# A linear-attention layer and two mixture-of-experts layers on one core: other steps, rows and counts in the attention stage

## The chip, the core and the metric

One core of one Trainium2 chip runs the whole program in one launch. The metric is device time in microseconds (us), the median of several runs. A core has five engines that run side by side, each with its own in-order list of instructions: TensorE (PE, matrix products), VectorE (DVE), ScalarE (ACT), GpSimd (POOL) and SyncE (SP, which here only starts transfers). An engine stops at an instruction whose inputs are not there, and everything behind it in its list stops too.

## What is computed

An attention with a decaying state is followed by a layer that sends each of 1536 tokens to the best of 8 experts, and by a second such layer with a capacity per expert.

```python
def _attn_ref(r, k, v, w, u):                      # 2 batches, 8 heads, 768 steps, 48 wide
    for t in range(S):
        cur = np.einsum('bhd,bhe->bhde', u[None] * kt, vt)
        y[:, :, t] = np.einsum('bhd,bhde->bhe', rt, state + cur)
        state = wt[:, :, :, None] * state + np.einsum('bhd,bhe->bhde', kt, vt)
...
def _moe_ref(x, ...):                              # 1536 x 384, 8 experts, 1024 hidden
    logits = x @ w_gate + modality_bias[modality_id]
    e_idx = np.argmax(logits, axis=1)
    ...
        h = np.maximum(x[mask] @ w1[e], 0.0)
        out[mask] = gate_w[mask, None] * (h @ w2[e])
```

## The kernel before, in words

**Attention.** The 16 heads are taken two at a time: 8 pairs (0 to 7), each of 6 chunks of 128 steps, so 48 chunk steps in all, one behind the other. For a pair, PE turns w, k and r (`turn`, three chunks to one PSUM tile, three such tiles in rotation); ACT copies w and r out of PSUM, DVE copies k out and multiplies it on the way (L270). DVE runs two scans over w: S (L282) and J (L290 to L292). r is multiplied by J (L297, `mul_r`) on the engine that the string `MR` names for the pair: v is DVE, g is POOL. POOL multiplies r, k and u (L321, L322) and later v (L329) for the diagonal term, whose sums DVE makes (L328).

For two chunks at a time `front` forms the products pa (L373, one PSUM tile only), and DVE masks them into Am (L376). For one chunk `out_y` adds the state's part (L415) and Am's part (L418) in PSUM, and DVE adds two chunks of it to zv (L421). `state` forms the next state: PE adds k times v (L391) in the PSUM tile endt. The string `STATE` says for each chunk of a pair how the old state X comes in. With p, PE adds it through a product with the identity (L393) and ACT scales the sum into the new X (L403). With v, DVE adds X to endt (Z, L398) and scales the sum (L401).

**Order.** All engines run in the order in which the code is written. The table `PLAN` says for each pair at which third of which chunk step each of its sixteen parts is written; `PRE`, `PLAN0` and `FRONT` do so for pair 0, with `F` and a number for that many products of ones (L524, `filler`), whose result nobody reads. `XTURN`, `XTURN2` and `XLOG` place the turns of finished rows and the expert logits of the first nine groups of 128 tokens; `SLOT` places single jobs.

**Choosing two experts early.** Once the first batch's logits are known, `Pick.find` counts its tokens per expert, finds the two experts with most tokens, and SP loads their weights while attention still runs (`RawWeights.first`, L966, L959, L961). Its DVE steps are written one or two to a chunk step (`pull`), from the chunk step `SLOT["pick"]` on.

**Behind attention** come the routing of the first expert layer (L785 on), that layer, a second routing and the second layer. Nothing there is touched by the change, but for the tiles that `Pick` hands over (`at`, `force`, `upto`, `hop`), which keep their meaning.

Of the kernel before, what the change touches and what calls it, by code (L numbers as in the profile page):

```python
# [59 lines left out]
XTURN = ((1, 0, 3, 5, 6, 7), (2, -2, 0, -1, 4, 4))  # L60
XTURN2 = ((2, 3, 4, 6, 7, 8), (2, 3, 5, 99, 99, 99))
# [68 lines left out]
class Pick:  # L130


    def __init__(self, nc, c, g, oh, psum):
        self.nc, self.c, self.oh, self.psum = nc, c, oh, psum
        self.T = lambda nm, shape, dt=F32: g.tile(shape, dt, name="pk_" + nm)
        self.one = []
        self.at = self.T("at", [1, 2])
        self.ati = self.T("ati", [1, 2], I32)

    def find(self):  # L140

# [9 lines left out]
        at = T("atm", [1, 2, E])  # L151
        num = c.jx[:, 0:E]
        for i in range(2):
            mx, eq, cum = T(f"mx{i}", [P, 1]), T(f"eq{i}", [P, E]), T(f"cum{i}", [P, E])
            one = T(f"one{i}", [P, E])
# [7 lines left out]
            self.one.append(one)  # L163
# [3 lines left out]
        a, b = self.one  # L167
# [1339 lines left out]
```

## Time and profile before

| | |
|---|---|
| median of 3 runs | 474.61 us (472.51 to 476.15) |
| the profiled execution's own time | 473.01 us, of which the profile's span is 471.3 us |
| PE busy | 429.7 us, 91% |
| DVE busy | 346.9 us, 74% |
| ACT busy | 239.4 us, 51% |
| POOL busy | 150.3 us, 32% |

Times in the views count from the start of the span. Attention runs from the start to about 128.8 us, the first routing to about 141.7 us, and the two expert layers to the end. A busy share says little by itself: PE's products take longer when its clock is granted at half, and then it is busy for longer with the same work. So the granted clock (PEclk, 1.00 for 2.4 GHz, 0.50 for 1.2 GHz) is read beside PE's list, and each gap in that list is read with what ended it.

### The profile page before, as it was taken

How to read it: one execution, taken by the hardware profiler on the slowest of the kernel's cores; microseconds unless marked ns; L12 is line 12 of the kernel's file. 1: busy time of each engine (PE TensorE's matmuls, PEld its weight loads, DVE VectorE, ACT ScalarE, POOL GpSimd, SP SyncE). 2: the span in 40 equal slices, each digit the busy share in tenths (PEclk: the TensorE clock that was granted, in tenths of full speed). 3: DMA queues.
4: the chain of work that ended last, by engine and by line, in shares of the span. 5: the costliest groups of instructions: out<-in, count | busy, mean ns of one | idle time of the engine just before them, and what ended most of it. 6: DMA issues, size and time to landing. Idle time of an engine off the chain costs nothing. (4 is left out here: it accounts for less than half of the span.)

```text
span 471.3 us, 9450 instructions
## 1 busy us (share of the span) xinstructions
PE 429.7 (91%) x3188; PEld 389.5 (83%) x3188; DVE 346.9 (74%) x669; ACT 239.4 (51%) x472; POOL 150.3 (32%) x159
## 2 busy tenths in 40 slices
PE   7989999979979899999999787898999999999990
PEld 4778878868739899999999776388899999998990
DVE  7787977994288984865947587889989559569770
ACT  3335353522344473654745464545857547568560
POOL 5528767230032032021220331243533221224500
PEclk9979999995799999999999889899999999999996
DMA  6966538108632022137772763431597676684200
GB/s 114 200 110 121 100 60 202 30 2 329 230 110 69 2 69 73 37 106 223 259 231 74 208 207 117 160 87 35 206 312 269 203 232 234 184 250 130 54 10 25
DMA packets 83989, 66.82 MB, mean 142 GB/s; under 512 B 58986, under 2 KB 76055, under 8 KB 83904
## 3 DMA queue, kind: packets, MB, share of 16 engines
q1 hardware_dynamic: 78912, 52.26, 37.4%
q0 software_dynamic: 4992, 13.53, 10.1%
q8 instruction: 42, 0.69, 0.6%
q14 instruction: 43, 0.35, 0.2%
HBM read 95.55 MB, written 11.51 MB: 227 GB/s over the span
## 5 line engine op out<-in xcount | busy, mean ns | idle before, releaser
L1007 DVE TENSOR_TENSOR w1l<-w1r,w1h 128x512 fp32r<-128x512 f32 x120 | 75.2, 683 | 0.8 <-ACT w1h L1004 0.7
L1007 DVE TENSOR_TENSOR w2l<-w2r,w2h 128x768 fp32r<-128x768 f32 x80 | 71.9, 949 | 0.7 <-ACT w2h L1004 0.5
L1004 ACT CAST w1h<-w1r 128x512 fp32r<-128x512 f32 x120 | 66.2, 621 | 7.2 <-DMA w2r<-in_moe_w_dram 6.2
L1004 ACT CAST w2h<-w2r 128x768 fp32r<-128x768 f32 x80 | 61.5, 838 | 0.0
L1133 ACT ACTIVATE qhh_m<-qh_m 128x512 fp32r<-128x512 f32 x48 | 28.7, 599 | 62.5 <-PE qh_m L1128 58.9
L1134 DVE SCALAR_TENSOR_TENSOR qhl_m<-qh_m,qhh_m 128x512 fp32r<-128x512 f32 x48 | 32.9, 686 | 28.4 <-ACT qhh_m L1133 27.8
L1128 PE MATMUL qh_m<-xh,w1h 128*128 128x256 f32 x288 | 51.6, 288 | 0.5 <-PE lpl_y_m L710 0.3
L1157 POOL DMA_INDIRECT x<-yo,ids_l x14 | 15.1, 1080 | 115.6 <-DVE yo L1154 66.0
L1128 PE MATMUL qh_m<-xl,w1h 128*128 128x256 f32 x288 | 50.2, 283 | 0.1
L1128 PE MATMUL qh_m<-xh,w1l 128*128 128x256 f32 x288 | 49.8, 282 | 0.0
L1157 POOL DMA_INDIRECT out_dram<-yo,ids_l x20 | 24.9, 1244 | 67.7 <-DVE w1l L1007 17.8
L1128 PEld LDWEIGHTS qh_m<-xh,w1h 128*128 128x128 f32 x288 | 42.3, 188 | 1.1 <-ACT xh L1337 0.8
L1046 POOL DMA_INDIRECT xg<-x,idg_l x24 | 28.1, 1170 | 45.8 <-PE xp_m L1061 32.4
L1128 PEld LDWEIGHTS qh_m<-xl,w1h 128*128 128x128 f32 x288 | 41.0, 189 | 0.5 <-DVE w2l L1007 0.5
L1128 PEld LDWEIGHTS qh_m<-xh,w1l 128*128 128x128 f32 x288 | 40.9, 188 | 0.0
L403 ACT ACTIVATE X<-endt,Sb 112x112 f32<-112x112 f32 x32 | 11.3, 354 | 50.9 <-PE endt L393 37.2
L1046 POOL DMA_INDIRECT xg<-xs,idg_l x20 | 22.7, 1136 | 34.9 <-DVE ec_l L888 29.1
L418 PE MATMUL py<-raw_v,Am 128*128 128x96 f32 x192 | 32.7, 299 | 0.0
L1062 ACT CAST xh<-xp_m 128x384 fp32r<-128x384 f32 x38 | 16.7, 485 | 27.9 <-PE xp_m L1061 26.6
L418 PEld LDWEIGHTS py<-raw_v,Am 128*128 128x128 f32 x192 | 29.5, 220 | 0.1
L1146 PE MATMUL qy_m<-w2h,qhh_m 128*128 128x384 f32 x96 | 25.6, 348 | 0.0
L1146 PE MATMUL y_m<-w2h,qhh_m 128*128 128x384 f32 x96 | 25.1, 342 | 0.0
(281 smaller groups left out, 964.7 us busy)
## 6 DMA issues: line engine op xcount, KB each, us to landing
w2r<-in_moe_w_dram SPq DMA_DIRECT2D x50, 768.0 KB
w1r<-in_moe_w_dram SPq DMA_DIRECT2D x72, 512.0 KB
xs<-zv SPq DMA_DIRECT2D x12, 192.0 KB
out_dram<-zt SPq DMA_DIRECT2D x4, 576.0 KB
raw_w<-in_w_dram SPq DMA_DIRECT2D x14, 144.0 KB
raw_r<-in_r_dram SPq DMA_DIRECT2D x14, 144.0 KB
raw_k<-in_k_dram SPq DMA_DIRECT2D x14, 144.0 KB
raw_v<-in_v_dram SPq DMA_DIRECT2D x14, 144.0 KB
```

The lines of the kernel that those rows point to most:

```text
L403: nc.scalar.activation(Xn, z, AF.Identity, scale=Tn)
L418: nc.tensor.matmul(py[:, 1 - h : 4 - h : 2, 0:D], lhsT=Am[:, h], rhs=vc[:, ch, :, 0:D], start=not ch, stop=True, skip_group_check=True)
L1004: (eng.copy if eng is nc.scalar else eng.tensor_copy)(p[1], p[0])
L1007: eng.tensor_sub(p[2], p[0], p[1].bitcast(F32))
L1046: nc.gpsimd.indirect_dma_start(out=m.xg[j % 2][:, t, 0:SW], out_offset=None, in_=src, in_offset=bass.IndirectOffsetOnAxis(ap=R.idg[:, 2 * ...
L1062: nc.scalar.copy(m.xh[j % 2][:, :, ts], pt)
L1128: nc.tensor.matmul(ph[:, f], lhsT=w[s][:, kc, fs], rhs=a[s][:, kc], start=(i == 0), stop=(i == 3 * KD - 1))
L1133: nc.scalar.activation(hh, ph, AF.Relu)
L1134: nc.vector.scalar_tensor_tensor(hl, ph, 0.0, hh.bitcast(F32), ALU.max, ALU.subtract)
L1146: nc.tensor.matmul(st["y", j, t], lhsT=a[:, f, ts], rhs=w[s][:, 2 * q + f], start=(q == 0 and i == 0), stop=(q == 3 and i == 5))
L1157: nc.gpsimd.indirect_dma_start(out=dst, out_offset=bass.IndirectOffsetOnAxis(ap=R.ids[:, 2 * j + t : 2 * j + t + 1], axis=0), in_=m.yo[j % ...
```

## The change

Five kinds of edit, all in the attention stage:

- `STATE` is ppppp in place of pppvp: for the fourth chunk of each of the 8 pairs, the old state comes in through PE and ACT and no longer through DVE.
- `MR` gives r times J of pairs 2, 4, 5 and 6 to DVE, and that of the others to POOL (before, pairs 1 to 7 were POOL's). Pair 0 is done on DVE in both.
- `Pick.find` joins count and expert number in one value (8 times the count plus the number), takes the two largest with one MAX and their places with one MAX_INDEX, and starts 5 chunk steps later. SP reads the places directly.
- The number and places of the products of ones: 35 in place of 32 for pair 0, and 3 more later.
- `PLAN`, `PRE`, `XTURN`, `XTURN2`, `XLOG` and `SLOT` write the same parts in another order.

```diff
 STEPS = ("w0", "w1", "r0", "S", "r1", "J", "k0", "mr", "k1", "mk", "K0", "K1", "u0", "u1", "c0", "c1")
-PLAN = {1: {'w0': -15, 'w1': -16, 'r0': -15, 'S': -15, 'r1': -13, 'J': -13, 'k0': -12, 'mr': -8, ...
+PLAN = {1: {'w0': -16, 'w1': -17, 'r0': -14, 'S': -16, 'r1': -12, 'J': -14, 'k0': -14, 'mr': -5, ...
-PRE = ('F6', 'n0', 'w0', 'w1', 'F0', 'A', 'S0', 'J0', 'r0', 'F0', 'A', 'm0', 'k0', 'S1', 'F8', 'r1', 'F2', 'J1', 'm1', 'K0', 'F1', 'k1', 'F6')
-FRONT = {0: 3, 1: 6}
-PLAN0 = {0: ('F0', 'n1', 'K1', 'F0', 'u', 'F0'), 3: ('A',), 1: ('U',), 10: ('c0',), 14: ('c1',)}
-MR = 'vggggggg'
-STATE = 'pppvp'
+PRE = ('F6', 'n0', 'w0', 'w1', 'F5', 'A', 'S0', 'J0', 'r0', 'F0', 'A', 'm0', 'k0', 'S1', 'F5', 'r1', 'F3', 'J1', 'm1', 'K0', 'F5', 'k1', 'F0')
+FRONT = {1: 7, 13: 2, 20: 1}
+PLAN0 = {0: ('F2', 'n1', 'K1', 'F0', 'u', 'F2'), 3: ('A',), 1: ('U',), 10: ('c0',), 14: ('c1',)}
+MR = 'ggvgvvvg'
+STATE = 'ppppp'
-SLOT = {'consts': 21, 'small': 9, 'pick': 27, 'xs': 29, 'flag': 44}
+SLOT = {'consts': 17, 'small': 10, 'pick': 32, 'xs': 26, 'flag': 44}
...
-        self.ati = self.T("ati", [1, 2], I32)
+        self.index = self.T("index", [P, 8], mybir.dt.uint32)
+        self.ati = self.index.bitcast(I32)
...
-        yield v.tensor_copy(n, pc)
...
-        for i in range(2):
-            yield v.tensor_reduce(mx, n, AX.X, ALU.max)
-            yield v.tensor_scalar(eq, n, mx, None, ALU.is_equal)
-            yield v.tensor_tensor_scan(cum, c.first[:, 0], eq, 0.0, ALU.mult, ALU.add)
-            yield v.scalar_tensor_tensor(one, cum, 1.0, eq, ALU.is_equal, ALU.mult)
-            if i == 0:
-                yield v.scalar_tensor_tensor(n, one, -2.0 * N, n, ALU.mult, ALU.add)
-            yield v.tensor_tensor(at[:, i], one[0:1], num[0:1], ALU.mult)
-        yield v.tensor_reduce(self.at, at, AX.X, ALU.add)
-        yield v.tensor_copy(self.ati, self.at)
+        yield v.scalar_tensor_tensor(n, pc, float(E), num, ALU.mult, ALU.add)
+        yield v.max(top, n)
+        yield v.max_index(self.index, top, n)
+        yield v.tensor_copy(self.at, self.index[0:1, 0:2])
         yield "at"
-        yield v.tensor_add(self.force, a, b)
-        yield v.tensor_sub(key, b, a)
+        yield v.tensor_scalar(self.force, n, top[:, 1:2], None, ALU.is_ge)
+        yield v.tensor_scalar(key, n, top[:, 0:1], None, ALU.is_equal)
+        yield v.scalar_tensor_tensor(key, n, top[:, 1:2], key, ALU.is_equal, ALU.subtract)
```

The lines of the changed kernel stand 9 lines higher behind `Pick.find` (L373 becomes L364).

**First place: PE, chunk steps 2 and 3 of pair 0.** In a name the digit is the pair (pk_1 is the turned k of pair 1); endt is the state, py the output. Before:

```order
L267 MATMUL pk_1_366<-ident,raw_k_113 112x128 x3
L415 MATMUL py_0_371<-X_0_311,rT_213 128x112
L418 MATMUL py_0_371<-raw_v_111,Am_0_285 128x2x48 x2
L391 MATMUL endt<-raw_v_111,KT_246 48x48 x2
L267 MATMUL pw_2_381<-ident,raw_w_116 112x128 x3
L267 MATMUL pw_2_386<-ident,raw_w_116 112x128 x3
L415 MATMUL py_0_371<-X_0_349,rT_213 128x112
L418 MATMUL py_0_371<-raw_v_111,Am_0_285 128x2x48 x2
L391 MATMUL endt<-raw_v_111,KT_246 48x48 x2
L393 MATMUL endt<-X_0_379,ident 112x112
L267 MATMUL pk_1_408<-ident,raw_k_113 112x128 x3
```

The same place in the changed kernel:

```order
L258 MATMUL pk_1_359<-ident,raw_k_113 112x128 x3
L258 MATMUL pr_1_369<-ident,raw_r_114 112x128 x3
L406 MATMUL py_0_378<-X_0_314,rT_218 128x112
L409 MATMUL py_0_378<-raw_v_111,Am_0_284 128x2x48 x2
L382 MATMUL endt<-raw_v_111,KT_249 48x48 x2
L384 MATMUL endt<-X_0_346,ident 112x112
L258 MATMUL pw_2_387<-ident,raw_w_116 112x128 x3
L258 MATMUL pw_2_392<-ident,raw_w_116 112x128 x3
L406 MATMUL py_0_378<-X_0_346,rT_218 128x112
L409 MATMUL py_0_378<-raw_v_111,Am_0_284 128x2x48 x2
L382 MATMUL endt<-raw_v_111,KT_249 48x48 x2
L384 MATMUL endt<-X_0_385,ident 112x112
```

The product with the identity now stands behind the first pair of L391 too. The next row in the changed kernel is the turn pk_1_409, whose PSUM tile was pk_1_359's.

**Second place: DVE at the same time.** Before:

```order
L292 SCALAR_TENSOR_TENSOR Jf_356<-wb_149,d1f_150 112x774
L270 TENSOR_TENSOR kT_365<-pk_1_366,Sb_333 112x384
L398 TENSOR_TENSOR Z_0_377<-endt,X_0_349 112x112
L401 TENSOR_SCALAR X_0_379<-Z_0_377,Sb_207 112x112
L421 TENSOR_TENSOR zv_156<-py_0_371,zv_156 128x2x96
L308 TENSOR_REDUCE ck<-Sb_207 112x1
L270 TENSOR_TENSOR kT_365<-pk_1_408,Sb_333 112x384
```

The same place in the changed kernel, up to the first Am of pair 1:

```order
L283 SCALAR_TENSOR_TENSOR Jf_354<-wb_149,d1f_150 112x774
L261 TENSOR_TENSOR kT_358<-pk_1_359,Sb_328 112x384
L412 TENSOR_TENSOR zv_156<-py_0_378,zv_156 128x2x96
L299 TENSOR_REDUCE ck<-Sb_212 112x1
L261 TENSOR_TENSOR kT_358<-pk_1_409,Sb_328 112x384
L273 SCALAR_TENSOR_TENSOR Sb_420<-wb_147,d1r 112x774
L367 TENSOR_TENSOR Am_1_438<-pa_1_433,mask 128x512
```

Z and X are gone from DVE; the scan S of pair 2 (L273) now stands ahead of pair 1's first Am.

**Third place: DVE from the second to the third Am of pair 6**, where the last pair's scan J and the choice of experts meet. Before:

```order
L376 TENSOR_TENSOR Am_6_1302<-pa_6_1297,mask 128x512
L290 TENSOR_SCALAR tcl_153<-Sb_1268 112x6
L291 RECIPROCAL d1f_150<-tcl_153 112x6
L292 SCALAR_TENSOR_TENSOR Jf_1308<-wb_149,d1f_150 112x774
L156 TENSOR_REDUCE pk_mx_1312<-pk_n 128x1
L157 TENSOR_SCALAR pk_eq_1313<-pk_n,pk_mx_1312 128x8
L158 SCALAR_TENSOR_TENSOR pk_cum_1314<-first,pk_eq_1313 128x8
L308 TENSOR_REDUCE ck<-Sb_1268 112x1
L421 TENSOR_TENSOR zv_157<-py_6_1317,zv_157 128x2x96
L159 SCALAR_TENSOR_TENSOR pk_one_1315<-pk_cum_1314,pk_eq_1313 128x8
L376 TENSOR_TENSOR Am_6_1345<-pa_6_1340,mask 128x512
```

In the changed kernel:

```order
L367 TENSOR_TENSOR Am_6_1279<-pa_6_1274,mask 128x512
L281 TENSOR_SCALAR tcl_153<-Sb_1265 112x6
L282 RECIPROCAL d1f_150<-tcl_153 112x6
L283 SCALAR_TENSOR_TENSOR Jf_1300<-wb_149,d1f_150 112x774
L261 TENSOR_TENSOR kT_1304<-pk_7_1305,Sb_1265 112x384
L153 SCALAR_TENSOR_TENSOR pk_n<-pk_pc,jx 128x8
L412 TENSOR_TENSOR zv_157<-py_6_1290,zv_157 128x2x96
L154 MAX pk_top<-pk_n 128x8
L367 TENSOR_TENSOR Am_6_1324<-pa_6_1318,mask 128x512
```

Between the scan and the last Am stood six small steps, four of them of the choice that read SBUF alone; now four steps stand there, of which one (MAX) reads SBUF alone.

## Rows read from the trace of the kernel before

**Rows 1.** Granted clock by stretch, attention: stretch, us, PE busy (count), PEclk, DMA

```profile
26.10:32.10 6.00, 6.00 (x31) 0.50 0.59 113
32.10:101.00 68.90, 65.75 (x666) 1.00 0.45 95
103.10:124.20 21.10, 20.64 (x118) 0.52 0.71 263
```

**Rows 2.** PE in time, first gap: start, duration, instruction [idle before <-releaser]

```profile
24.84 0.29 PE L391 MATMUL endt<-raw_v,KT 128*48 128x48 f32 x4 [2.12 <-DVE Z L398]
26.10 0.72 PE L393 MATMUL endt<-X,ident 112*112 112x112 f32 x2 [0.97 <-DVE X L401]
```

**Rows 3.** DVE in time, ahead of the first gap's end

```profile
24.07 0.53 DVE L270 TENSOR_TENSOR kT<-pk,Sb 112x384 f32<-112x384 f32 x1
24.52 0.26 DVE L398 TENSOR_TENSOR Z<-endt,X 112x112 f32<-112x112 f32 x1
24.82 1.23 DVE L401 TENSOR_SCALAR X<-Z,Sb 112x112 f32<-112x112 f32 x1
```

**Rows 4.** POOL in time, at the first gap

```profile
24.30 1.68 POOL L297 TENSOR_TENSOR rT<-rT,Jf 112x768 f32<-112x768 f32 x1 [2.21 <-DMA raw_v<-in_v_dram]
```

**Rows 5.** PE in time, second gap

```profile
103.10 0.71 PE L373 MATMUL pa<-rT,kT 48*128 48x128 f32 x8 [2.08 <-DVE Am L376]
104.28 0.40 PE L391 MATMUL endt<-raw_v,KT 128*48 128x48 f32 x4 [0.46 <-DVE Z L398]
```

**Rows 6.** DVE in time, ahead of the second gap's end

```profile
97.35 1.77 DVE L292 TENSOR_TENSOR_SCAN Jf<-wb,d1f 112x774 f32<-112x774 f32 x1
...
99.47 1.53 DVE L158 TENSOR_TENSOR_SCAN pk_cum<-first,pk_eq 128x8 f32<-128x8 f32 x1
...
101.26 1.10 DVE L159 SCALAR_TENSOR_TENSOR pk_one<-pk_cum,pk_eq 128x8 f32<-128x8 f32 x1
102.28 0.68 DVE L376 TENSOR_TENSOR Am<-pa,mask 128x512 f32<-128x512 f32 x1
```

**Rows 7.** POOL in time, at the second gap

```profile
99.26 1.71 POOL L297 TENSOR_TENSOR rT<-rT,Jf 112x768 f32<-112x768 f32 x1 [6.29 <-DVE pk_mx L156]
100.93 1.40 POOL L321 TENSOR_TENSOR z<-raw_r,raw_k 128x576 f32<-128x576 f32 x1
102.41 1.40 POOL L322 TENSOR_TENSOR z<-z,ub 128x576 f32<-128x576 f32 x1
```

**Rows 8.** PE in time: another gap, and the longest with no fall behind it

```profile
134.79 1.02 PE L860 MATMUL pid_l<-rid_l,ohp_l 128*128 128x26 f16 x12 [1.53 <-DVE ohp_l L858]
277.48 0.47 PE L1080 MATMUL ph_m<-w1h,xh 128*128 128x512 f32 x1 [1.95 <-ACT w1h L1004]
```

**Rows 9.** Granted clock behind the gap that ends at 277.48

```profile
278.00:280.00 2.00, 2.00 (x6) 0.50 0.58 116
```

**Rows 10.** PE in time: two products at the full clock, then at half

```profile
97.42 0.72 PE L373 MATMUL pa<-rT,kT 48*128 48x128 f32 x8
100.43 0.60 PE L418 MATMUL py<-raw_v,Am 128*128 128x96 f32 x4
107.20 1.03 PE L418 MATMUL py<-raw_v,Am 128*128 128x96 f32 x4
108.16 1.23 PE L373 MATMUL pa<-rT,kT 48*128 48x128 f32 x8
```

**Rows 11.** PE in time: products of ones, a product with the identity, its successor

```profile
7.14 1.89 PE L524 MATMUL junk<-fill 128*128 128x512 bf16 x8
...
16.42 0.45 PE L393 MATMUL endt<-X,ident 112*112 112x112 f32 x2
16.70 0.82 PE L267 MATMUL pw<-ident,raw_w 128*112 128x128 f32 x6
```

**Rows 12.** DVE in time: half a pair's r times J, pair 0

```profile
8.01 0.56 DVE L297 TENSOR_TENSOR rT<-rT,Jf 112x384 f32<-112x384 f32 x1
```

**Rows 13.** SP in time: the first load of the chosen experts' weights

```profile
106.11 1.44 SPq L959 DMA_DIRECT2D w1r<-in_moe_w_dram  x3
```

More of the change, by code (lines that the diff above doesn't have):

```diff
@@ new lines @@
+PLAN = {1: {'w0': -16, 'w1': -17, 'r0': -14, 'S': -16, 'r1': -12, 'J': -14, 'k0': -14, 'mr': -5, 'k1': -8, 'mk': -9, 'K0': -6, 'K1': -1, 'u0': -12, 'u1': -4, 'c0': 0, 'c1': 8}, 2: {'w0': -28, 'w1': -27, 'r0': -25, 'S': -24, 'r1': -20, 'J': -22, 'k0': -18, 'mr': -10, 'k1': -10, 'mk': -5, 'K0': -11, 'K1': -1, 'u0': -13, 'u1': -3, 'c0': -9, 'c1': 3}, 3: {'w0': -26, 'w1': -33, 'r0': -26, 'S': -24, 'r1': -19, 'J': -20, 'k0': -16, 'mr': -17, 'k1': -12, 'mk': -11, 'K0': -7, 'K1': 1, 'u0': -16, 'u1': -7, 'c0': -14, 'c1': 0}, 4: {'w0': -33, 'w1': -28, 'r0': -23, 'S': -21, 'r1': -15, 'J': -19, 'k0': -15, 'mr': -9, 'k1': -6, 'mk': -11, 'K0': -14, 'K1': -2, 'u0': -8, 'u1': -4, 'c0': 2, 'c1': 5}, 5: {'w0': -27, 'w1': -31, 'r0': -17, 'S': -22, 'r1': -13, 'J': -15, 'k0': -21, 'mr': -13, 'k1': -5, 'mk': -11, 'K0': -7, 'K1': 0, 'u0': -23, 'u1': -9, 'c0': -12, 'c1': 3}, 6: {'w0': -32, 'w1': -25, 'r0': -23, 'S': -23, 'r1': -22, 'J': -20, 'k0': -20, 'mr': -18, 'k1': -19, 'mk': -11, 'K0': -8, 'K1': -6, 'u0': -20, 'u1': -13, 'c0': -11, 'c1': -10}, 7: {'w0': -29, 'w1': -32, 'r0': -26, 'S': -22, 'r1': -20, 'J': -16, 'k0': -16, 'mr': -10, 'k1': -12, 'mk': -11, 'K0': -14, 'K1': -6, 'u0': -10, 'u1': -1, 'c0': -14, 'c1': -5}}
@@ L57 @@
+FRONT = {1: 7, 13: 2, 20: 1}
+PLAN0 = {0: ('F2', 'n1', 'K1', 'F0', 'u', 'F2'), 3: ('A',), 1: ('U',), 10: ('c0',), 14: ('c1',)}
+MR = 'ggvgvvvg'
+STATE = 'ppppp'
 KD_ = 'dddddddd'
 AHEAD = (3, 1)
-SLOT = {'consts': 21, 'small': 9, 'pick': 27, 'xs': 29, 'flag': 44}
-XTURN = ((1, 0, 3, 5, 6, 7), (2, -2, 0, -1, 4, 4))
-XTURN2 = ((2, 3, 4, 6, 7, 8), (2, 3, 5, 99, 99, 99))
+SLOT = {'consts': 17, 'small': 10, 'pick': 32, 'xs': 26, 'flag': 44}
+XTURN = ((-3, -1, 2, 8, 4, 5), (0, 3, 2, -1, 0, 5))
+XTURN2 = ((2, 3, 4, 8, 6, 5), (5, 1, 4, 99, 99, 99))
@@ L65 @@
 GROUPS = ((0, (0, 1, 2)), (0, (3, 4, 5)), (1, (0, 1, 2)))
-XLOG = (4, 8, 5)
+XLOG = (4, 9, 5)
 EXPERT0 = (0, E - 1)
@@ L135, in __init__ @@
         self.T = lambda nm, shape, dt=F32: g.tile(shape, dt, name="pk_" + nm)
-        self.one = []
         self.at = self.T("at", [1, 2])
-        self.ati = self.T("ati", [1, 2], I32)
+        self.index = self.T("index", [P, 8], mybir.dt.uint32)
+        self.ati = self.index.bitcast(I32)
     def find(self):
         v, c, T = self.nc.vector, self.c, self.T
-        n = T("n", [P, E])
-        yield v.tensor_reduce(n, self.oh[:, :, 0:CH], AX.X, ALU.add)
         half = T("half", [P, E], BF16)
-        yield v.tensor_copy(half, n)
+        with self.nc.allow_low_precision(reason="whole numbers up to six"):
+            ins = v.tensor_reduce(half, self.oh[:, :, 0:CH], AX.X, ALU.add)
+        yield ins
         yield
@@ L149, in find @@
         yield self.nc.tensor.matmul(pc, lhsT=c.ones, rhs=half, start=True, stop=True)
-        yield v.tensor_copy(n, pc)
-        at = T("atm", [1, 2, E])
         num = c.jx[:, 0:E]
-        for i in range(2):
-            mx, eq, cum = T(f"mx{i}", [P, 1]), T(f"eq{i}", [P, E]), T(f"cum{i}", [P, E])
-            one = T(f"one{i}", [P, E])
-            yield v.tensor_reduce(mx, n, AX.X, ALU.max)
-            yield v.tensor_scalar(eq, n, mx, None, ALU.is_equal)
-            yield v.tensor_tensor_scan(cum, c.first[:, 0], eq, 0.0, ALU.mult, ALU.add)
-            yield v.scalar_tensor_tensor(one, cum, 1.0, eq, ALU.is_equal, ALU.mult)
-            if i == 0:
-                yield v.scalar_tensor_tensor(n, one, -2.0 * N, n, ALU.mult, ALU.add)
-            yield v.tensor_tensor(at[:, i], one[0:1], num[0:1], ALU.mult)
-            self.one.append(one)
-        yield v.tensor_reduce(self.at, at, AX.X, ALU.add)
-        yield v.tensor_copy(self.ati, self.at)
+        n, top = T("n", [P, E]), T("top", [P, 8])
+        yield v.scalar_tensor_tensor(n, pc, float(E), num, ALU.mult, ALU.add)
+        yield v.max(top, n)
+        yield v.max_index(self.index, top, n)
+        yield v.tensor_copy(self.at, self.index[0:1, 0:2])
         yield "at"
-        a, b = self.one
         self.force = T("force", [P, E])
-        yield v.tensor_add(self.force, a, b)
+        yield v.tensor_scalar(self.force, n, top[:, 1:2], None, ALU.is_ge)
         key = T("key", [P, E])
-        yield v.tensor_sub(key, b, a)
+        yield v.tensor_scalar(key, n, top[:, 0:1], None, ALU.is_equal)
+        yield v.scalar_tensor_tensor(key, n, top[:, 1:2], key, ALU.is_equal, ALU.subtract)
         yield v.scalar_tensor_tensor(key, key, 2.0 * E, num, ALU.mult, ALU.add)
```

1 line of the change is left out of this document (removed).

## The prediction

> **What bounds the kernel now.** I read the granted clock by stretch first, then PE's own list in order of time with the gap ahead of each row, and then, for each long gap, the lists of the engines that it names. Attention is a stretch of small products on PE, one behind the other, and PE is what it waits for: from 32.10 to 101.00 us PE is busy for 65.75 of 68.90 us at the full clock [rows 1]. Two stretches are different. From 26.10 to 32.10 and from 103.10 to 124.20 us PE is as busy, but at a granted clock of 0.50 and 0.52, half speed [rows 1]. Ahead of each stands a gap. In the first PE waits 2.12 us for Z and then 0.97 us for X, the two DVE steps that bring the old state in [rows 2]. In the second it waits 2.08 us for an Am and then 0.46 us for a Z [rows 5].
>
> A gap costs its own length and, if it is long, the clock behind it. In the whole trace PE has five gaps of 1.95 us and more, and each is followed by half speed (for the shortest, at 277.48 us, the clock is 0.50 just behind it). The longest that isn't is 1.53 us [rows 8, 9]. At half speed the masked product of L418 takes 1.03 us where it took 0.60, and pa 1.23 where it took 0.72 [rows 10]. That is 1.71 times as long, so of each us at half speed 0.41 is lost (1 less 1/1.71). The two stretches hold 6.00 and 20.64 us of busy time [rows 1] and lose 2.5 and 8.5 us. With the gaps (2.12 + 0.97 + 2.08 + 0.46 = 5.6 us) that is 16.6 us of attention's 128.8 in which PE does less than it could.
>
> Why DVE is late is in the lists of DVE and POOL. DVE steps that read SBUF alone, with two inputs or as a plain scale, stand still while POOL multiplies. At 99.47 us an 8-wide scan takes 1.53 us, until POOL's r times J (99.26 us, 1.71 us) is done. The next such step at 101.26 us takes 1.10 us, until POOL's next product (100.93 us, 1.40 us) is done [rows 6, 7]. At 24.82 us the scale of Z takes 1.23 us beside POOL's r times J at 24.30 us [rows 3, 4]. Steps with a PSUM input don't wait: Am at 102.28 us takes 0.68 us although the next POOL product starts at 102.41 us [rows 6, 7].
>
> **First gap.** The change takes Z and X off DVE for all 8 pairs, so PE no longer needs DVE between two chunks. What is late next at this place is kT of pair 1: the turn of its second half goes into the PSUM tile of the first, which DVE reads from 24.07 to 24.60 us [rows 3]. Nothing of DVE's work ahead of it changes, so it stays at 24.60. PE came to the old gap at 24.84 - 2.12 = 22.72 us [rows 2] with the same turns done. In the changed order it has in addition two products with the identity and one pair of L391 to do before it stops (0.28 us each from the start of one to the start of its successor, 16.42 to 16.70 us [rows 11], and no more for the other), 0.8 us, and three more products of ones, 0.65 us (0.216 us each, the start-to-start step in 1.89 us for eight, less the 0.16 us by which the last one ends late [rows 11]). It arrives at about 24.2 us and waits 0.4 us. A little later pa of chunks 2 and 3 of pair 1 needs the Am ahead of it, which now stands behind pair 2's scan S. That scan has to wait for POOL's r times J until 25.98 us [rows 4], takes 1.77 us as J does [rows 6], and Am 0.68: 28.4 us. PE, with six more groups of products of 0.3 to 0.7 us behind 24.6, comes there at about 27.7 and waits 0.7 us. Both waits are short, so no half speed is to follow.
>
> **Second gap.** Between the end of the last pair's scan J (97.35 + 1.77 = 99.12 us) and Am (102.28 us) DVE spent 3.2 us, of which 2.6 in two 8-wide steps held up by POOL [rows 6, 7]. In the changed order four steps stand there: kT (0.53, as at 24.07 us [rows 3]), one that reads PSUM, the sum into zv, and MAX. Only MAX reads SBUF alone. No row shows a MAX: from below it is an 8-wide step of 0.15 us (the 0.6 us that the two held steps leave of the 3.2, over four steps), from above it is held until POOL's r times J ends, as the scan at 99.47 us was, 1.53 us. I take the upper value, because POOL starts that product as soon as J is done. Then Am ends 2.5 us behind the scan, 1.3 us earlier than now (102.96 less 99.12 = 3.8). PE stopped 1.9 us behind the scan (103.10 - 2.08 = 101.02); it now has one product with the identity and one of ones more to do there (0.5 us). On that count alone 0.1 us is left to wait, and DVE, freed of the choice's steps between the Ams of pair 6, enters the stretch without the backlog that it had (Am at 102.28 belongs to a pa that was done at 98.14 us [rows 6, 10]). So the gap goes.
>
> **The other parts.** Eight products with the identity more, on PE, in plain sight: 8 x 0.28 = 2.2 us. Six more products of ones: 6 x 0.216 = 1.3 us; those of pair 0 lie partly in its waits, so the bounds are 0 and 1.3, and I take 1.3. ACT gets eight scales more, as it has them for the other chunks; it is busy for 51% of the span, and each scale has a chunk step's time until its X is read. DVE gets r times J of four pairs: 0.56 us for half a pair [rows 12], so about 1.0 for one, 4 us, against eight times Z and X (0.26 us for Z [rows 3] and, where nothing holds it, as much for X, 4.2 us) and ten steps of the choice (0.15 each, 1.5 us). So DVE has 1.7 us less, and POOL 4 x 1.68 = 6.7 us less [rows 4]. The rest of `PLAN` moves parts by one or two chunk steps; I went through the order pair by pair with these durations and found no wait above 1 us. Turns, logits and stores are as many as before. The choice starts five chunk steps later but has eleven writings less, so the load of the weights is issued at the same place within half a chunk step: 106.11 us now [rows 13], 22.7 us ahead of attention's end. At the full clock it would come about 18 us ahead of that end. Eight transfers, 4.7 MB, are wanted by then, the first five of them first. At the 263 GB/s of the stretch in which they run now [rows 1], a rate that counts time without loads too, they take 18 us at most. That cover gets thin but holds; without it each us late is a us lost.
>
> By a rule of the Trainium skill (GPSIMD Engine Reference, section 8, Key points) GpSimd shares its SBUF interfaces with VectorE and is in contention with its instructions that have two SBUF inputs. The trace agrees, with 1.53 us for an 8-wide scan. It speaks against the four multiplies on DVE: by it each can be held for a POOL product, and the sum would be 4 x 1.40 = 5.6 us worse on DVE. PE would see only what exceeds its lead.
>
> **Sum.** 16.6 us of gaps and half speed go; 2.2 for products with the identity, 1.3 for products of ones and 1.1 for the two new waits come: 12.0 us less. Against the profiled execution's own 473.01 us that is 461.0. The median of the runs is 474.61, 1.6 above it, so 462.6 us. Nothing behind attention changes, and the gain is handed through to the end, since routing and the expert layers start when the last logits are there.
>
> **Rivals.** *One long gap is left.* DVE or POOL is late at one more place, most likely where DVE has r times J of pair 6 behind scan J and two kT (about 4.8 us of DVE work between two Ams, against 3.5 us of PE work), or at MAX, if POOL's three products run through without letting it in (4.5 us [rows 7]). For it: POOL's products did hold DVE through. Against it: DVE comes to both places with a lead, as the sums above show for MAX. The rule on the shared interfaces, in the Trainium skill's page named above, would bring this case about. Its price is a gap of 2 us and half speed for 6.0 to 20.6 us, 2 + 2.5 to 2 + 8.5 us: 467 to 473 us. *The waits only move.* Both gaps return in another form, because steps taken from DVE let others come up that wait as long: then 3.5 us of new PE work stand against nothing, and the time is 473 to 478 us. Against it: the two steps that PE waited for are off its path or 1.3 us earlier. *Slower.* Am of pair 1 behind scan S is late by more than 1.95 us and not by 0.7, since POOL's r times J and the scan run one behind the other. The clock falls at about 28 us, in front of 90 us of small products like those in which it stayed at half for 21 us. From 29 us at half speed on (12.0/0.41) the gain is gone; 45 us would give 462.6 + 2 + 18 = 483 us. Against it: after the first gap the clock was back after 6 us.
>
> **How the numbers follow.** Both gaps gone: 0.63, around 462.6 us, from 457.5 (new waits and ones hidden, and the run like the profiled one) to 466.5. One long gap left: 0.24, 467 to 473. The waits only move: 0.08, 473 to 478. Slower: 0.05, 479 to 490. The range that leaves out some 2 in 10 is 457.5 to 471.5 us. A difference of 1%, 4.7 us, is about what a measurement of this kernel can tell from no change. Faster by over 1% means below 469.9 us: all of the first case and half of the second, 0.74. Within 1%: 0.2. Slower by over 1%: 0.06.
>
> **What would show it.** In the changed profile PE's gap at about 24 us is below 1 us and the clock stays at 1.00 behind it; the gap ahead of pair 7's first pa is below 1 us and the clock stays at 1.00 to the end of attention; the last logits are there at about 117 us and not at 128.8; MAX ends with POOL's r times J or before; the stretch from attention's end to the end of the span is as long as now, 342.5 us. I am wrong if a PE gap of 2 us stands anywhere in attention, or if ACT or PE waits for the weights of the first two experts behind it.

## The result, and the profile after

The changed kernel takes 459.0 us (median of 4 runs, 457.5 to 465.7) where the kernel before, beside it, takes 475.3 us: a ratio of 0.968, 95% interval 0.961 to 0.974. The ratio goes by the fast executions alone, so it leaves out the one of 465.7 us and takes in a further one of 462.1 us. The profiled execution is the longest of the four, 465.7 us with a span of 464.0 us; it has two waits in the second expert layer, to which the last section comes back.

The clock row of the page, one digit for each fortieth of the span, first before, then after:

```profile
PEclk9979999995799999999999889899999999999996
```

```profile
PEclk9999999999899999999997997999999999997995
```

Before, the 7 in the third place (23.6 to 35.3 us) and the 5 and 7 behind the ninth (106 to 130 us) are attention's half speed. After, attention has none up to 112 us; the 8 in the eleventh place is the routing behind it. By the page PE, DVE, ACT and POOL are busy for 425.9, 335.6, 241.9 and 142.4 us, against 429.7, 346.9, 239.4 and 150.3 us before.

The clock by stretch, from attention's first gap to its end (columns as in [rows 1], with PE alone):

```profile
24.00:28.30 4.30, 3.71 (x33) 1.00 0.74 87
28.30:95.83 67.53, 66.47 (x679) 1.00 0.49 103
95.83:112.40 16.57, 15.62 (x164) 1.00 1.00 369
```

From 24 us to the end of attention the clock is 1.00, where [rows 1] have 0.50 and 0.52 in two stretches. PE's rows that answer to [rows 2, 5] (start, duration, instruction, idle time before it and what ended it), with pair 0's first pa and the product that transposes the last logits:

```profile
11.92 0.72 PE L364 MATMUL pa<-rT,kT 48*128 48x128 f32 x8
...
24.68 0.54 PE L258 MATMUL pk<-ident,raw_k 128*112 128x128 f32 x3 [0.31 <-DVE kT L261]
28.26 0.71 PE L364 MATMUL pa<-rT,kT 48*128 48x128 f32 x8 [0.29 <-DVE Am L367]
...
95.83 0.72 PE L364 MATMUL pa<-rT,kT 48*128 48x128 f32 x8
...
112.06 0.30 PE L466 MATMUL endt<-ident,lq 96*128 96x96 f32 x1 [0.35 <-ACT lq L463]
```

The 2.12 us and 0.97 us of the first gap are 0.31 and 0.29 us now; the pa of pair 7 at 95.83 us has no wait at all, where it had 2.08 us. Two rows of the kernel before stand against the first and the last of these:

```profile
12.50 0.72 PE L373 MATMUL pa<-rT,kT 48*128 48x128 f32 x8
...
128.52 0.30 PE L475 MATMUL endt<-ident,lq 96*128 96x96 f32 x1 [0.35 <-ACT lq L472]
```

The last logits come 128.52 - 112.06 = 16.5 us earlier. With [rows 5] this divides into three stretches: up to the first pa 12.50 and now 11.92 us; from there to pair 7's first pa 90.60 (103.10 - 12.50) and now 83.91 us; from there to the last logits 25.42 and now 16.23 us. The gains are 0.6, 6.7 and 9.2 us.

DVE and POOL at the place of [rows 6, 7], after:

```profile
90.29 1.77 DVE L283 TENSOR_TENSOR_SCAN Jf<-wb,d1f 112x774 f32<-112x774 f32 x1
...
92.77 0.16 DVE L154 MAX8 pk_top<-pk_n 128x8 f32<-128x8 f32 x1
92.84 0.67 DVE L367 TENSOR_TENSOR Am<-pa,mask 128x512 f32<-128x512 f32 x1
...
93.57 0.16 DVE L155 FIND_INDEX8 pk_index<-pk_top,pk_n 128x8 uint32<-128x8 f32 x1
...
94.50 0.79 DVE L156 CAST pk_at<-pk_index 1x2 f32<-1x2 uint32 x1
```

```profile
92.21 1.68 POOL L288 TENSOR_TENSOR rT<-rT,Jf 112x768 f32<-112x768 f32 x1 [6.34 <-DVE Jf L283]
```

MAX takes 0.16 us in the middle of POOL's r times J, and FIND_INDEX8 as much; neither is held. The Am ends at 93.51 us, 1.45 us behind the scan's end (92.06).

### The profile page after: what moved, and what is told of

Same layout as the page of the kernel before. It is cut to its first block, busy times and chain, and to the rows that moved or that the text cites. A ratio compares the mean times of both kernels' runs of the same rounds, so it can differ in the third digit from the quotient of the medians.

```text
span 464.0 us, 9459 instructions
## 1 busy us (share of the span) xinstructions
PE 425.9 (92%) x3205; PEld 384.6 (83%) x3210; DVE 335.6 (72%) x648; ACT 241.9 (52%) x480; POOL 142.4 (31%) x155
## 5 line engine op out<-in xcount | busy, mean ns | idle before, releaser
L1037 POOL DMA_INDIRECT xg<-x,idg_l x24 | 26.9, 1120 | 55.2 <-PE xp_m L1052 35.9
L394 ACT ACTIVATE X<-endt,Sb 112x112 f32<-112x112 f32 x40 | 14.1, 353 | 38.4 <-PE endt L384 27.1
L409 PE MATMUL py<-raw_v,Am 128*128 128x96 f32 x192 | 28.5, 271 | 0.0
L1071 PE MATMUL ph_m<-w1h,xh 128*128 128x256 f32 (+1 forms) x54 | 20.1, 372 | 8.8 <-issue 5.0
L409 PEld LDWEIGHTS py<-raw_v,Am 128*128 128x128 f32 x192 | 25.4, 191 | 0.1
```

Source lines behind the costliest of these rows:

```text
L394: nc.scalar.activation(Xn, z, AF.Identity, scale=Tn)
L409: nc.tensor.matmul(py[:, 1 - h : 4 - h : 2, 0:D], lhsT=Am[:, h], rhs=vc[:, ch, :, 0:D], start=not ch, stop=True, skip_group_check=True)
L1037: nc.gpsimd.indirect_dma_start(out=m.xg[j % 2][:, t, 0:SW], out_offset=None, in_=src, in_offset=bass.IndirectOffsetOnAxis(ap=R.idg[:, 2 * ...
L1071: nc.tensor.matmul(ph[:, q * wd : q * wd + wd], lhsT=a[s][:, kc, P:], rhs=w[s][:, kc, hs], start=(i == 0), stop=(i == 3 * KD - 1))
```

## Experiments

Labels with b start from the kernel before, labels with a from the changed kernel. The time of the last logits is given beside the whole time, since it leaves out what happens behind attention. The theory is the prediction's: PE's long gaps cost their length and the half speed behind them, and what counts is which DVE steps POOL holds up ahead of the ones that PE waits for.

**Is the half speed due to the gap?** `b_ones` adds products of ones where PE idles and takes no wait away (`idle` gives them a PSUM tile of their own).

```diff
             i, ch = d // 3, d % 3 * 2
+            if d == 21:                      # ahead of pair 7's first pa
+                idle(9, "f")
...
             how = STATE[ch]
+            if g == 4:                       # ahead of the L391 that waits for Z
+                idle(9, "s")
...
+            if g == 4:                       # ahead of the L393 that waits for X
+                filler(4, st["s"])
...
```

> The kernel before with 22 products of ones more and nothing else: nine ahead of the L391 that waits for Z and four ahead of the L393 that waits for X at the first gap, nine ahead of the pa that waits for an Am at the second. They fill time in which PE idles (0.216 us each, 4.7 of 5.6 us) and take none of the waits away. Theory (half speed comes from the idle time ahead of it): the clock stays at 1.00 behind both places, 2.5 and 8.5 us less, 464 us, while the waits stay where they were. Rival one (half speed comes from the kind of products that follow): clock 0.5 at 26 to 32 and 103 to 124 us as before, 474 to 476 us. Rival two (the ones stand in the way of the waiting products): 476 to 480 us.

```profile
22.87 2.11 PE L530 MATMUL idle_s<-fill 128*128 128x512 bf16 x8
25.16 0.29 PE L395 MATMUL endt<-raw_v,KT 128*48 128x48 f32 x4 [0.18 <-DVE Z L404]
```

```profile
26.00:32.00 6.00, 6.00 (x57) 1.00 0.66 103
103.00:117.00 14.00, 13.41 (x145) 1.00 0.85 315
```

The first fence is PE in time, the second the clock by stretch. The waits are where they were (L395 still starts when Z is there), but the clock stays at 1.00, and the last logits are there at 117.80 us: 10.7 us earlier with 22 products more, against 11.0 worked out. So at these two places there is no half speed without the idle time, and the kind of products behind it is not the cause. The whole time gains less: 469.5 us (463.8 to 473.1), ratio 0.988 [0.983, 0.993]; in the profiled execution the part behind attention is 5.0 us longer than before (347.8 against 342.8, last section).

**Which part of the new choice counts?** `b_pick` puts the new `Pick.find` into the kernel before, at its old chunk step; `b_pick32` starts it five chunk steps later. The second differs from the first by one number.

```diff
-SLOT = {..., 'pick': 27, ...}
+SLOT = {..., 'pick': 32, ...}                # b_pick32 alone; both have the new Pick.find
```

> The kernel before with the new choice of experts alone, started at the same chunk step as the old one. It has eleven DVE writings less, but behind the last pair's scan J stand three steps of the rest of the choice that read SBUF alone (key, upto, nxt), two or three of them beside POOL's r times J and its products. Theory (it counts which steps POOL holds there, not how many there are in all): the second gap stays at about 2 us and half speed with it, first gap unchanged, 473 to 476 us. Rival (fewer steps of the choice are the gain): second gap gone, 464 us.

> The kernel before with the new choice, and started five chunk steps later as in the changed kernel; all else as before. Behind scan J of the last pair only MAX then reads SBUF alone ahead of the Am. Theory: second gap below 1 us, clock 1.00 to the end of attention, first gap and its half speed unchanged: 2.1 + 8.5 us less, 464 to 465 us. Rival (the order of everything else is needed too): 472 to 476 us.

DVE of `b_pick` behind the last pair's scan J (which ends at 101.87 us):

```profile
102.69 1.05 DVE L170 TENSOR_SCALAR pk_nxt<-pk_rank 1x8 f32<-1x8 f32 x1
103.67 0.67 DVE L367 TENSOR_TENSOR Am<-pa,mask 128x512 f32<-128x512 f32 x1
104.27 0.90 DVE L172 TENSOR_TENSOR pk_is<-pk_rank,pk_nxt 1x64 f32<-1x64 f32 x1
105.20 1.44 DVE L173 TENSOR_TENSOR pk_is<-pk_is,jx 1x64 f32<-1x64 f32 x1
```

and its PE:

```profile
104.49 0.71 PE L364 MATMUL pa<-rT,kT 48*128 48x128 f32 x8 [0.65 <-DVE Am L367]
106.88 0.40 PE L382 MATMUL endt<-raw_v,KT 128*48 128x48 f32 x4 [1.68 <-DVE Z L389]
```

Ten DVE steps less (the prediction counted eleven; the edit takes out 18 and puts in 8), and nothing is won: three steps of at most 64 elements take 1.05, 0.90 and 1.44 us, the gap of 2.08 us became 0.65 and 1.68 us, and from 107 to 126 us the clock is 0.50. The last logits come at 131.20 us, 2.7 us later than before; at 87.94 us PE also waits 1.42 us for the choice's own first sum (pk_half), with the clock at 0.50 from 89.6 to 93.0 us. Three of four runs took 475.2 to 478.4 us; the fourth took 465.9 us at a mean clock of 0.977 where the profiled one has 0.948, so in that one the clock seems to have held (no trace of it was kept). `b_pick32`:

```profile
99.27 0.16 DVE L154 MAX8 pk_top<-pk_n 128x8 f32<-128x8 f32 x1
99.35 0.67 DVE L367 TENSOR_TENSOR Am<-pa,mask 128x512 f32<-128x512 f32 x1
```

Only MAX stands ahead of the Am, pair 7's first pa starts at 101.53 us with no wait, the clock is 1.00 to the end of attention, and the last logits are there at 117.56 us, 11.0 us earlier (10.6 expected). 463.6 us (461.8 to 463.8), ratio 0.981 [0.973, 0.990]. So with the new form the later place alone brings 11.0 of attention's 16.5 us. No run starts the old form at chunk step 32, so whether the shorter form is needed for that isn't shown.

**What is STATE worth?** `b_state` changes that string alone; `b_both32` adds the late choice.

```diff
-STATE = 'pppvp'
+STATE = 'ppppp'                              # b_state; b_both32 is b_pick32 with this line
```

> The kernel before with STATE ppppp alone: the old state comes in through PE and ACT for all chunks. Theory: at the first gap PE no longer waits for Z and X but about 1 us for the PSUM tile that kT of pair 1 reads until 24.6 us, and the clock stays at 1.00: 5.6 us of gap and clock less, 1.0 us more. Eight products with the identity cost 8 x 0.28 = 2.2 us. The second gap keeps its 2.1 us and its half speed, since the choice of experts still stands there. Last logits at 125.5 to 126 us, time 470 to 471 us. Rival (DVE without Z and X catches up in pair 7 too): second gap below 1.5 us, 460 us.

> The kernel before with STATE ppppp and the new choice five chunk steps later, and neither the new order nor the other engines for r times J nor the other products of ones. Theory (two gaps, two causes, and the two add up): last logits at 128.5 - 2.6 - 11 = 115 us, time 460 to 461 us; what then is left to the 112 us of the changed kernel is what the new order is worth. Rival (the order is needed for both): a PE gap of 2 us or more in attention, 465 us or more.

```profile
26.46 0.54 PE L267 MATMUL pk<-ident,raw_k 128*112 128x128 f32 x3 [1.10 <-DVE kT L270]
27.83 1.23 PE L373 MATMUL pa<-rT,kT 48*128 48x128 f32 x8 [0.83 <-POOL rT L297]
```

```profile
27.80:45.00 17.20, 17.17 (x98) 0.51 0.61 119
108.74:128.50 19.76, 19.76 (x114) 0.52 0.76 280
```

These are `b_state`'s PE rows and clock. It is slower: 479.7 us (479.1 to 481.0), ratio 1.015 [1.010, 1.020], last logits at 134.06 us. I had not seen the second of the two waits: with Z and X gone PE runs into r times J of pair 1, which POOL has not done yet. The clock falls all the same and stays down for 17 us. `b_both32` has the same two waits:

```profile
24.83 0.54 PE L258 MATMUL pk<-ident,raw_k 128*112 128x128 f32 x3 [1.12 <-DVE kT L261]
26.20 0.87 PE L364 MATMUL pa<-rT,kT 48*128 48x128 f32 x8 [0.83 <-POOL rT L288]
```

```profile
26.20:30.00 3.80, 3.80 (x23) 0.56 1.02 188
30.00:45.00 15.00, 15.00 (x152) 1.00 0.61 119
```

but there the clock is back after 4 us: last logits at 115.70 us (115 expected), 462.2 us, ratio 0.976 [0.971, 0.981]. So STATE in the old order brought 1.9 us in the one (117.56 - 115.70) and lost 5.5 us in the other (134.06 - 128.52). Of the 5.5 us, 1.8 lie ahead of the first pa (14.31 us against 12.50), which the edit doesn't touch: in this execution the clock rose later, and the eight products of ones at the start take 3.30 us where they took 1.89 [rows 11]. Why half speed lasted 17 us in the one and 4 in the other isn't settled by these runs. What lies between `b_both32` and the changed kernel, 3.6 us (115.70 - 112.06), belongs to the new order, to `MR` and to the products of ones together; no run has the order alone.

`a_state` undoes STATE in the changed kernel.

```diff
-STATE = 'ppppp'
+STATE = 'pppvp'
```

> The changed kernel with STATE put back to pppvp, so that Z and X are on DVE again for the fourth chunk of each pair. Theory: behind kT of pair 1 DVE does Z, then X, which POOL's r times J holds until 26.0 us, and only then the scan S of pair 2 and the Am behind it. PE waits some 1.2 us for Z, 0.9 us for X and 1.3 to 2 us for that Am instead of 0.5 and 0.7 us, with half speed behind one of them; it has eight products with the identity (2.2 us) less. Last logits at 115 to 120 us, time 462 to 468 us. Rival (STATE costs what it brings, the order alone is the gain): 457 us.

```profile
24.88 0.29 PE L382 MATMUL endt<-raw_v,KT 128*48 128x48 f32 x4 [1.32 <-DVE Z L389]
26.15 0.45 PE L384 MATMUL endt<-X,ident 112*112 112x112 f32 x2 [0.97 <-DVE X L392]
```

```profile
26.15:45.00 18.85, 17.96 (x177) 1.00 0.71 136
```

The two waits came as worked out (1.2 and 0.9 us), but the third did not exceed 0.6 us and the clock held; further on PE waits 0.73 and 1.12 us for r times J on DVE. Last logits at 114.30 us, 2.2 us later than with STATE ppppp; 460.4 us (457.3 to 467.5), ratio 0.973 [0.964, 0.982]. Neither theory had it right: STATE is worth 2.2 us here, not the 3 to 8 us of the theory, and not nothing, as the rival had it. In the whole time the two kernels can't be told apart (460.4 us against 459.0 and 462.8).

**The old choice in the new order.** `a_oldpick` takes the old `Pick.find` back and starts it at chunk step 27.

```diff
-SLOT = {..., 'pick': 32, ...}
+SLOT = {..., 'pick': 27, ...}                # and the old Pick.find
```

> The changed kernel with the old choice of experts, started at the old chunk step. Behind scan J of the last pair its 8-wide scan and product stand ahead of the Am again, beside POOL's r times J and product. Theory: the two are held 1.4 and 1.3 us, Am ends at about 96 us and not at 93.5, PE comes to that pa at 95.8, so it waits 0.3 us only and the clock stays at 1.00: 459 to 462 us. The steps of the choice are a cost only where PE has no lead. Rival (the form of the choice is the gain): gap of 2 us, half speed to the end of attention, 470 us.

```profile
93.78 1.48 DVE L158 TENSOR_TENSOR_SCAN pk_cum<-first,pk_eq 128x8 f32<-128x8 f32 x1
...
95.44 1.18 DVE L159 SCALAR_TENSOR_TENSOR pk_one<-pk_cum,pk_eq 128x8 f32<-128x8 f32 x1
96.55 0.68 DVE L376 TENSOR_TENSOR Am<-pa,mask 128x512 f32<-128x512 f32 x1
```

```profile
97.37 0.71 PE L373 MATMUL pa<-rT,kT 48*128 48x128 f32 x8 [0.46 <-DVE ck L308]
```

The two steps are held again, 1.48 and 1.18 us, and PE waits 0.46 us (put down to the reduction ck right behind the Am), since in the new order it comes later to this pa. The clock stays at 1.00, last logits at 113.75 us, as the theory has it. The time is 465.3 us (464.5 to 465.6), ratio 0.983 [0.979, 0.988], above the 459 to 462 expected: again by what is lost behind attention.

**The price of a delay, set by hand.** `a_late1` and `a_late2` put four or six reductions ahead of one Am of the changed kernel.

```diff
+            if d == 11:
+                for x in range(4):                       # six in a_late2
+                    nc.vector.tensor_reduce(late[:, x : x + 1], d1r, AX.X, ALU.max)
             nc.vector.tensor_mul(Am, sc, ...)
```

> The changed kernel with four reductions of 112x774 (some 0.9 us each by the 0.75 us of the 128x576 one) ahead of the Am at 54.7 us, whose results nobody reads. That Am is awaited by a pa at 58.3 us, so it has 2.85 us of lead. Theory (DVE's delay costs only what exceeds the lead, and a short gap costs its own length): a PE gap of some 0.7 us at 59 us, clock 1.00 behind it, last logits 0.5 to 1 us later than 112, 460 us. Rival (any delay of DVE shows at the end): 3.5 us later.

> The same with six reductions. Theory: a PE gap of some 2.5 us at 59 us and half speed behind it, as at the second gap of the kernel before: the gap and 0.41 us for each us at half speed, of which there may be 4 to 21 us, so last logits 4 to 11 us later than 112 us, 463 to 470 us. Rival (a gap costs its own length alone): 2.5 us later, 461.5 us.

PE of the first, then of the second, each with its clock behind the gap:

```profile
60.14 0.71 PE L365 MATMUL pa<-rT,kT 48*128 48x128 f32 x8 [2.01 <-DVE rT L289]
```

```profile
60.14:70.00 9.86, 9.46 (x104) 1.00 0.38 112
```

```profile
61.24 1.01 PE L365 MATMUL pa<-rT,kT 48*128 48x128 f32 x6 [3.12 <-DVE rT L289]
```

```profile
61.24:67.80 6.56, 6.35 (x45) 0.50 0.00 0
```

The gaps are 1.3 and 0.6 us longer than worked out, because the pa waits for r times J, which DVE does behind the Am. In the first the clock held through a gap of 2.01 us, and the last logits come 1.8 us later (113.90 us): the gap alone. In the second the gap is 3.12 us, the clock is 0.50 for 6.56 us with 6.35 us of busy time, and they come 5.8 us later (117.84); gap and half speed by the prediction's price are 3.12 + 0.41 x 6.35 = 5.7 us. Times 464.2 us, ratio 0.982 [0.975, 0.989], and 469.4 us, ratio 0.991 [0.988, 0.994].

**The two terms that I took on guess.** `a_ones` takes products of ones away (eight: two, three and three; the "six" of its text is a slip), `a_mr` gives r times J of pairs 2, 4, 5 and 6 back to POOL.

```diff
-FRONT = {1: 7, 13: 2, 20: 1}
+FRONT = {1: 5}                                           # a_ones
-PLAN0 = {0: ('F2', 'n1', 'K1', 'F0', 'u', 'F2'), ...
+PLAN0 = {0: ('F0', 'n1', 'K1', 'F0', 'u', 'F1'), ...     # a_ones
-MR = 'ggvgvvvg'
+MR = 'vggggggg'                                          # a_mr
```

> The changed kernel with six products of ones less (two fewer ahead of chunk pair 1 of pair 0, three at its start, and the three later ones ahead of pairs 4 and 6 gone, one moved). My sum had them as 1.3 us of PE time in plain sight. If that holds: last logits at 110.8 us. If they lie in waits: 112 us, no change. If they keep the clock up: a stretch at 0.50 in the first 40 us or behind 62 or 91 us, 114 us or more.

> The changed kernel with r times J of pairs 2, 4, 5 and 6 back on POOL, one instruction of 1.68 us each in place of one of 0.95 us on DVE. Theory: DVE has 4 us less, POOL 6.7 us more at 32% busy, neither is what PE waits for, so nothing moves by more than 1 us, unless the product comes too late for its pa, which PE waited 0.6 us for in the kernel before: last logits at 112 to 113.5 us, 458 to 461 us. Rival (by the skill's page on GpSimd the shared SBUF interface makes the four products on DVE dear): 3 us earlier without them. Second rival (POOL holds DVE for longer, so Ams are late): a gap of 2 us, 465 us or more.

In `a_ones` eight products (1.7 us) are gone, and PE waits 0.90 us for kT where it waited 0.31, and 0.76 us for the first Am where it waited 0.30. Last logits at 111.63 us, 0.4 us earlier. So these ones lie mostly in waits, and they weren't needed to hold the clock. Its time is 456.3 us (456.2 to 456.5), ratio 0.964 [0.961, 0.967], the lowest of all; the interval overlaps that of the change itself, so that it beats the changed kernel is likely and not shown. `a_mr` has the last logits at 112.97 us, 0.9 us later, with a wait of 0.77 us for POOL's r times J at 36.8 us; 462.2 us, ratio 0.976 [0.972, 0.979]. The four multiplies on DVE bring a little, by sparing that wait; the rival, by which they would be dear there, didn't come, and they take 0.95 us each.

**A second look at the change.** `a_again` is the changed kernel as it is.

> The changed kernel once more, for a second profiled execution. Its first one took 465.7 us where the other runs took 457.5 to 462. My theory has all of the gain in attention, so: last logits at 112 us again (128.5 before), no PE gap of 1.95 us or more before them, and behind them as long as before, 342 to 345 us and not the 351 of the first profiled execution. Time 459 us. The rival, that something is also lost for good behind attention (the weights are loaded in a shorter time), expects 350 us there again.

Last logits at 111.75 us, no gap of 1.95 us before them, 462.8 us (459.8 to 467.0), ratio 0.977 [0.966, 0.988]. But behind attention its profiled execution takes 353.4 us of 465.2, as the rival had it. The rival's reason, the loading of the weights, isn't shown: the waits there are others (last section).

## Why the prediction was right, and where it was not

**What bounds it: right.** Attention's two gaps and the half speed behind them were the loss. Filling the idle time gave 10.7 us (`b_ones`, 11.0 worked out), removing the second gap alone 11.0 (`b_pick32`, 10.6 by 2.1 + 8.5).

**The cause on DVE: right.** Steps of 8 to 64 elements took 0.90 to 1.53 us beside POOL's products in three kernels ([rows 6], `b_pick`, `a_oldpick`), and ten fewer of them brought nothing at the old place (`b_pick`), while a later place brought 11.0 us (`b_pick32`).

**First gap: right in kind, the waits too high.** kT is next, 0.31 us (0.4 forecast). The wait for the Am behind pair 2's scan is 0.29 us and not 0.7. I had the scan start when POOL's product ends; it started at once and was longer by 0.13 us than J:

```profile
25.73 1.90 DVE L273 TENSOR_TENSOR_SCAN Sb<-wb,d1r 112x774 f32<-112x774 f32 x1
```

**Second gap: right in kind, wrong for MAX.** I took the upper end, 1.53 us; it is 0.16 us (`b_pick32` as well). The Am ends 1.45 us behind the scan and not 2.5. By the rule of the Trainium skill that the prediction named (GPSIMD Engine Reference, section 8, Key points) the contention is with instructions that have two SBUF inputs or run in a 2-port performance mode. MAX has one input and wasn't held, so the trace agrees. A conversion of two elements, also with one input, took 0.79 us, to the end of POOL's next product (the CAST at 94.50); whether it ran in such a mode no run shows.

**The sum: 12.0 us forecast, 16.5 us in attention.** By the three stretches the last one went as worked out (8.5 + 0.46 less 0.28, 8.7, against 9.2). The middle one should have brought 3.3 us (5.6 and 2.1 of waits and half speed, less 7 x 0.28, 1.3 and 1.1) and brought 6.7. PE's list of that stretch, before and after:

```profile
12.50:103.10 90.60, 82.28 (x795) 0.96 0.53 106
```

```profile
11.92:95.83 83.91, 81.79 (x816) 1.00 0.58 116
```

PE's idle time falls from 8.32 to 2.12 us. The gaps' 5.17 us (2.12 + 0.97 + 2.08) are gone, and the new waits add up to what was forecast, by luck: 1.06 us of idle time up to 28.30 us (0.31 and 0.29 us, and 0.46 us at two places right behind the first pa that the sum does not have) against 1.1. One term was missing. Between 32.10 and 101.00 us PE idled 68.90 - 65.75 = 3.15 us [rows 1]; from 28.30 to 95.83 us it now idles 67.53 - 66.47 = 1.06 us. That is 2.1 us of small waits that are gone, the longest of them 0.62 us for POOL's r times J at 50.45 us and 0.78 us for kT at 61.65 us, and my sum held the order of the rest at nothing. The other 1.3 us are in busy time: by the sum it should have grown by 0.8 us (7 x 0.28 + 1.3 - 2.5), and it fell by 0.5 (82.28 - 81.79). Why the products take less than the sum has them isn't settled. The price of the ones was too high in its own right (`a_ones`: eight of them 0.4 us), but they fill the idle time counted here, so this isn't to be added. The 0.6 us ahead of the first pa I had not counted either.

**DVE's multiplies, the weights: right.** In the changed kernel no wait above 0.6 us came with the multiplies, and without them it is 0.9 us worse (`a_mr`); with Z and X on DVE as well (`a_state`) one of them was waited for, 1.12 us. The weights were issued 17.6 us ahead of attention's end (18 forecast), and ACT begins to convert them 0.3 us behind the last logits; the wait ahead of that is put down to a store (xs) and not to them:

```profile
94.77 1.45 SPq L950 DMA_DIRECT2D w1r<-in_moe_w_dram  x3
```

```profile
112.33 3.21 ACT L995 CAST w1h<-w1r 128x512 fp32r<-128x512 f32 x6 [0.32 <-DMA xs<-zv]
```

**Behind attention: forecast as long as now, 342.5 us; half right.** `a_ones` has 343.0 us, `a_state` 341.8, but the two profiled executions of the changed kernel 351.9 and 353.4. So the forecast of 462.6 us was 3.6 us above the median by two errors of opposite sign, and that it came so near is partly luck: attention's gain was 4.5 us too small, and the 0.9 us that the median run loses elsewhere, if its attention gained the same 16.5 us (474.6 - 16.5 = 458.1, against 459.0), was not in it. With the loss of the profiled execution, 9.1 us (351.9 - 342.8), more than half of attention's gain is used up.

**The rivals.** "One long gap is left" didn't come, and its rule for the price held (`a_late2`). But the premise that a gap of 1.95 us decides was too simple, as the next section but one shows. "Slower" got 0.05, on the ground that waits of 0.4 and 0.7 us are short. `b_state` shows how near it was: two waits of 1.10 and 0.83 us at that very place, with 17 us of half speed behind them, made the kernel slower than before. The changed kernel has 0.31 us and no wait for these two; that the new order is what spares them is likely and not shown, since eight products of ones less bring the first back to 0.90 us (`a_ones`).

## What to carry to other kernels

Price a gap of PE together with the granted clock behind it, and try first what products of ones in the idle time give: here 10.7 of attention's 16.5 us, with no other edit. Where POOL and DVE both work from SBUF, don't count the small steps but look where they stand: an 8-wide scan or product ahead of the step that PE waits for cost 1.1 to 1.5 us while POOL multiplied, where MAX, as wide, cost 0.16. And an edit that removes a wait should be run in the order that it will live in, since STATE alone made the kernel slower (ratio 1.015).

## What the runs showed of the hardware

**When the clock falls.** At the same place PE idled 2.12 + 0.97 us (before: half speed for 6 us), 1.10 + 0.83 us (`b_state`: 17 us), 1.12 + 0.83 us (`b_both32`: 4 us) and 1.32 + 0.97 us (`a_state`: none). A gap of 1.73 us in `b_state` cost 20 us at half speed, one of 2.01 us in `a_late1` none. The longest gap with no fall behind it is 2.91 us, in the first expert layer of `a_ones`; its row and the clock behind it:

```profile
247.88 0.47 PE L1071 MATMUL ph_m<-w1h,xh 128*128 128x512 f32 x1 [2.91 <-ACT w1h L995]
```

```profile
247.88:260.00 12.12, 11.01 (x77) 1.00 0.95 308
```

Nor is the clock back as soon as PE is busy: in `b_state` PE idles nowhere from 108.74 to 128.50 us, and the clock stays at 0.52. So the length of one gap doesn't decide by itself; what does, besides, these rows don't show. By the Trainium skill (TensorE: Matmul & The Clock Gate, Part 1) the monitor's window runs freely and isn't tied to the kernel; that would let like gaps end differently, and no run here tests it.

**PE stands still for nothing that the profile shows.** In the second expert layer of the changed kernel, PE in time, and the clock behind it:

```profile
421.12 0.76 PE L1071 MATMUL ph_m<-w1h,xh 128*128 128x512 f32 x1 [3.69 <-issue]
```

```profile
420.00:427.00 7.00, 5.88 (x19) 0.51 0.06 21
```

and the same place in `a_ones`, where that product starts with no wait:

```profile
415.01 0.40 PE L1071 MATMUL ph_m<-w1h,xh 128*128 128x512 f32 x1
```

Such a wait of 1.3 to 1.4 us and, 92 to 93 us later, one of 2.4 to 3.9 us (in `b_ones` put down to ACT's conversion, in most with half speed behind it) stand in the profiled executions of `a_again`, `b_ones`, `a_oldpick`, `a_late1`, `a_late2`, `a_mr` and the changed kernel, and their part behind attention is 347 to 353 us long. The kernel before, `b_pick`, `b_pick32`, `b_state`, `b_both32`, `a_state` and `a_ones` have neither, and 342 to 345 us. In the kernel these products stand behind a branch, in the Else arm of `with tc.If(kd > 0)`. By the pages the seven with the waits run 3204 to 3210 PE instructions and the seven without 3184 to 3204; only attention's part differs between them. By the Trainium skill (Runtime: NRT & Kernel Launch, Instruction fetch mechanics) a taken branch out of the part of the program at hand waits for its code to be fetched. The traces agree so far as they go: in all fourteen waits a packet of 16 KB on the queue that the page calls instruction (q8) ends 1.3 to 1.7 us before PE goes on. In the changed kernel it ends at 419.54 us and PE goes on at 421.12; in `a_ones` the like packet starts at 415.10 us, when PE has begun already. But no run changed the length of the list and nothing else, and the list alone can't decide: the other three timed runs of the changed kernel took 457.5 to 459.2 us, so they can't have lost as much. So the cause stays open. If it is the fetch, a few instructions in attention move up to 10 us elsewhere, and that would be the larger part of what sets `a_ones` apart.
